# Where ScalarE makes a weight piece's top bits: between d and gh, or behind the piece's rounding

## The chip, the cores and the metric

The kernel runs on one core of one Trainium2 chip. The metric is the device time of one launch in microseconds (us). The three runs of the kernel before took 845.73, 847.87 and 848.03 us, the median is 847.87 us. The names of the engines are those of the profile: PE is TensorE, DVE is VectorE, ACT is ScalarE, POOL is GpSimd, SP is SyncE, whose queue issues the loads.

## The reference

Three layers follow one another, all in float32. The first is attention with a decay instead of a softmax; the second a feed-forward layer with the activation h·tanh(softplus(h)); the third sends each of the 2304 tokens to one of eight experts with a fixed capacity.

```
ret = (scale * q @ k.T) * Dmat ; x = ret @ v          # 4 x 8 heads, 576 x 64
h = x @ w_in                                          # 2304 x 512 @ 512 x 2048
g = h * tanh(log1p(exp(h))) ; y = g @ w_out           # 2048 -> 512
out[mask_e] = relu(y[mask_e] @ w1[e]) @ w2[e]         # 8 experts, 288 tokens each
```

## The kernel before, in words

Float32 products are made of split halves: a high part rounded to the matmul format (names ending in h) and the rest (ending in l), so each product is three matmuls. The second layer works in steps. A step is one block of 256 tokens (n) and one 128-wide slice f of the 2048 hidden units; there are 144 steps (9 blocks of 16 slices). In step i the program issues, in the order in which it is written:

- TensorE: twelve matmuls of h into the PSUM tile ph (L317), pieces of the attention that `slots` puts on this step (steps 0 to 9 carry many), and at the end the six matmuls of the output for the step three before (L411).
- ScalarE: tanh, square and scaling of ph into d (L326, L327, L328), and gh, the rounded high part of the activated value of the step two before (L358).
- VectorE: a product r of the two halves of d (L334), gl, the rest of gh (L359), a reciprocal (L339), u of the step before times ph (L352), and u of this step (L344). While weights are being made gl is on VectorE, later on GpSimd.

In the first 31 steps the weights of the second layer are also made, one piece of 128x512 a step. There are 32 pieces, half from w_in (winh, winl) and half from w_out (woh, wol). A piece arrives as 64-bit words (tile raw), and passes through six instructions of the class `convert`:

- `x1` on ScalarE, L159: makes the piece's top bits in the lower words of raw.
- `c` on ScalarE, L156: copies the upper word, scaled, into one of two buffers (y0).
- `x` on VectorE, L163: puts the sign into the top bits.
- `a` on VectorE, L168: joins top bits and copy. Behind it `fetch` issues the load of a later piece (L140, on SP's queue) into the raw buffer that has become free; raw has two buffers for most pieces, so it is the piece two further on.
- `h` on ScalarE, L174: the rounding, which gives the high part of the weights.
- `l` on GpSimd, L177: the rest.

A piece begins with `x1` and `c` in one step, has `x`, `a` and `h` in the next, and `l` in the one after (in the program; GpSimd starts it when the rounding is done). So a step's ScalarE work belongs to two pieces: `h` of one (`now`), `x1` and `c` of the next (`nxt`). No piece begins in step 20. Four pieces (0 to 3) begin ahead of the loop, 28 inside it. Each engine works through its own queue in order. Other VectorE work in the steps with attention is pm (L224) and xl (L255), other GpSimd work are two products on att (L228, L233), other ScalarE work xh (L254) and sd (L285).

Of the kernel before, what the change touches and what calls it, by code (L numbers as in the profile page):

```python
# [57 lines left out]
CONV = [i for i in range(80) if i < ALL or int((i + 1) * RATE) > int(i * RATE)]  # L58
# [23 lines left out]
def first_part(ctx, tc, att, att_ht, att_hn, dtab, qtab, ktab, stab, wi, wo, wgb, ydram, L, constants, cst, begin, grid):  # L82
# [59 lines left out]
    class convert:  # L142
# [18 lines left out]
        def x(self):  # L161
            w0 = self.w0
            nc.vector.scalar_tensor_tensor(w0, self.w1, 0x80000000, w0, op0=ALU.bitwise_and,  # L163
                                           op1=ALU.bitwise_or)
# [144 lines left out]
    def ff_h(n, f, i):  # L309
        xh, xl = x_block(n)  # L310
        if i % 2 == 0:
            hbank[0] = psum.tile([P, 2, TB], F32, tag=("ph0", "ph1")[i // 2 % 2], name="ph")
        ph = hbank[0][:, i % 2, :]
        k = 0
        for kt in range(KT):
            for w, x in ((winh, xh), (winl, xh), (winh, xl)):
                nc.tensor.matmul(ph, w[f][:, kt, :], x[:, kt, :], start=(k == 0), stop=(k == 11))  # L317
                k += 1
        q2[n, f] = ph

    def ff_a1(n, f, i, alone):

        ph = q2[n, f]
        d = work.tile([P, 2, P], F32, tag="d", name="d", bufs=2)
        df = d.rearrange("p a b -> p (a b)")
        nc.scalar.activation(df, ph, AF.Tanh, scale=0.5)  # L326
        nc.scalar.activation(df, df, AF.Square, bias=half_b, scale=-0.5)  # L327
        nc.scalar.activation(df, df, AF.Copy, bias=0.5, scale=0.5)  # L328
        u = work.tile([P, 2, P], F32, tag="u", name="u", bufs=3)
        r = u[:, 0, :]  # L330
        if alone:

            r = work.tile([P, DM], BF, tag="scr", name="r").bitcast(F32)[:, :P]
        nc.vector.tensor_mul(r, d[:, 0, :], d[:, 1, :])  # L334
        inv[n, f] = (d, u, r, alone)

    def ff_a2(n, f):
        r = inv[n, f][2]
        nc.vector.reciprocal(r, r)  # L339

    def ff_b1(n, f, eng):
        d, u, r, alone = inv.pop((n, f))
        if alone:
            eng.tensor_mul(u, d[:, ::-1, :], r[:, None, :].to_broadcast([P, 2, P]))  # L344
        else:
            eng.tensor_mul(u[:, 1, :], d[:, 0, :], r)  # L346
            eng.tensor_mul(u[:, 0, :], d[:, 1, :], r)  # L347
        gt[n, f] = u.rearrange("p a b -> p (a b)")

    def ff_b2(n, f):  # L350
        g = gt[n, f]
        nc.vector.scalar_tensor_tensor(g, g, -1.0, q2.pop((n, f)), op0=ALU.add, op1=ALU.mult)  # L352

    def ff_b3(n, f, eng):
        g = gt[n, f]
        gh = work.tile([P, TB], F32R, tag="gh", name="gh", bufs=3)
        gl = work.tile([P, TB], F32R, tag="gl", name="gl", bufs=3)
        nc.scalar.activation(gh, g, AF.Copy)  # L358
        eng.tensor_sub(gl, g, gh.bitcast(F32))  # L359
        gt[n, f] = (gh, gl)  # L360
# [152 lines left out]
    old, now, nxt = c2, c3, convert()  # L513
# [17 lines left out]
    for i in range(len(steps) + YL):  # L531
        new = i < len(steps)
        if i == 20:
            constants()
        if i == 62:
            stage.__exit__(None, None, None)
            late = tc.tile_pool(name="late", bufs=1)
            WG = late.__enter__().tile([P, E, DM], F32, name="WG")
            nc.sync.dma_start(WG, wgb)
        if now:  # L540
            now.x()
            now.a()
        if old:
            old.l()
        if new:
            n, f = steps[i]
            ff_h(n, f, i)
            for x in slots.get(i, []):
                x()
            ff_a1(n, f, i, bool(now or old))  # L550
        if nxt and i in CONV:
            nxt.x1()
        if new:

            eng = nc.vector if now or old else nc.gpsimd
            if i > 1:
                ff_b3(*steps[i - 2], eng)
            ff_a2(n, f)
            if i:
                ff_b2(*steps[i - 1])  # L560
            ff_b1(n, f, nc.vector if i == len(steps) - 1 else eng)
        if i == len(steps) - 1:
            ff_b2(n, f)
            ff_b3(*steps[i - 1], nc.gpsimd)
            ff_b3(n, f, nc.vector)
        if now:
            now.h()
        old, now = now, None
        if nxt and i in CONV:
            now, nxt = nxt, convert() if done[0] < len(parts) else None  # L570
            now.c()
        for k in range(2 if i % 4 == 0 or TAIL <= i < POP2 else 1):
            if idle:
                idle.pop(0)()
        if late and i > TAIL + BEGIN and not idle:
            late = late.__exit__(None, None, None)
            soon.extend(begin())
        if i >= YL:
            ff_y(*steps[i - YL], i)
# [840 lines left out]
def build(tc, ap, out):  # L1420
    nc = tc.nc
    with ExitStack() as ctx:
        pp = ctx.enter_context(tc.tile_pool(name="pp", bufs=1))
        dp = ctx.enter_context(tc.tile_pool(name="dp", bufs=1, space=bass.MemoryType.DRAM))
        cp = ctx.enter_context(tc.tile_pool(name="cp", bufs=1))
        ctx.enter_context(tc.manual_schedule())
        L = pp.tile([P, NT, E], F32, name="L")
        ydram = dp.tile([N, DM], F32, name="ydram")
        cst = {}
        start = []  # L1430
        cs = ExitStack()

        def begin():
            start.append(Search(cs, tc, L, cst))
            return start[0].early()

        with ExitStack() as c1:
            first_part(c1, tc, ap["att"], ap["att_ht"], ap["att_hn"], ap["dtab"], ap["qtab"],
                       ap["ktab"], ap["stab"], ap["wi"], ap["wo"], ap["wgb"], ydram, L, lambda: constants(cp, tc, ap, cst), cst, begin, lambda *a: Grid(cs, tc, L, cst).pieces(*a))
        keep = ctx.enter_context(tc.tile_pool(name="keep", bufs=1, reuse_waits="tile"))  # L1440
        L0 = keep.tile([P, NT, E], F32, name="L0")
        nc.gpsimd.tensor_copy(L0, L)
        with ExitStack() as c2:
            flag = second_part(c2, tc, L, ydram, ap["wx"], cst, out, start[0], True, L0)
            again = nc.values_load(flag[0:1, 0:1], min_val=0, max_val=1)
        cs.close()
        with tc.If(again != 0):
            with ExitStack() as c3:
                general_constants(c3, tc, ap, cst)
                second_part(c3, tc, L0, ydram, ap["wx"], cst, out, Start(c3, tc, L0, cst), False)  # L1450
# [15 lines left out]
def constants(cp, tc, ap, cst):  # L1466
    nc = tc.nc
    load_constants(cp, tc, ap, cst, (("ident", [P, P], F32), ("J", [P, NJ + 1], F32), ("SCL", [P, 3], F32),
                                     ("pri", [P, E], F32), ("tri", [P, P], BF), ("io", [P, 96], BF),
                                     ("pcv", [P, NT, 2], BF), ("WGN", [P, KT, E], F32)))  # L1470
    cst["ones"] = cp.tile([P, P], BF, name="c_ones")
    nc.vector.memset(cst["ones"], 1.0)
# [69 lines left out]
```

## Time and profile before

| | us |
|---|---|
| median of three runs | 847.87 |
| profiled execution, its own time | 849.51 |
| its span in the trace | 847.60 |
| PE busy | 776.6 (92%) |
| DVE busy | 548.1 (65%) |
| ACT busy | 437.3 (52%) |
| POOL busy | 475.1 (56%) |
| first and last L159 begin | 10.3, 156.3 |

Busy shares are means over the span. The stage in which weights are made is the first fifth of it, and there VectorE is the busiest engine, not TensorE. From the span's start to 170 us, DVE was busy for 135.67 us and PE for 134.16 us; behind that PE is busy nearly all the time.

### The profile page before, as it was taken

What the parts mean: (1) busy time and instruction counts of PE and PEld (TensorE: products, weight loads), DVE (VectorE), ACT (ScalarE), POOL (GpSimd) and SP (SyncE); (2) the same over time, 40 slices, a digit from 0 to 9 for tenths busy, and PEclk for the clock granted to TensorE, in tenths of its full rate; (3) what the DMA queues carried; (4) which work ended last, traced back from release to release, by engine and by line L of the source; (5) the groups of instructions that cost most, each with busy time, mean ns of one, the idle gap of its engine ahead of it and who ended that gap; (6) DMA issues with size and microseconds to landing.
All of it is one profiled execution on the core that took longest, in us unless ns stands there. A gap on an engine that the chain in (4) does not pass through costs nothing.

```text
span 847.6 us, 16248 instructions
## 1 busy us (share of the span) xinstructions
PE 776.6 (92%) x6151; PEld 709.3 (84%) x6151; DVE 548.1 (65%) x1271; ACT 437.3 (52%) x963; POOL 475.1 (56%) x541
## 2 busy tenths in 40 slices
PE   6688878899999999999999999939999999999993
PEld 5677667788998888888888889929989899999993
DVE  4797989865545699797897885576566654442110
ACT  2677878754554545455455554423444543554520
POOL 2533333365544567676666665414777986977811
PEclk9799999999999999999999999958999999999997
DMA  8536343101204210120110000044555655655411
GB/s 313 174 111 201 137 135 125 50 27 51 75 26 150 76 50 26 61 82 34 51 50 26 1 26 2 2 147 163 171 181 178 194 168 174 177 159 175 128 30 32
DMA packets 27320, 87.63 MB, mean 103 GB/s; under 512 B 4448, under 2 KB 5600, under 8 KB 27104
## 3 DMA queue, kind: packets, MB, share of 16 engines
q1 hardware_dynamic: 24160, 77.06, 27.9%
q0 software_dynamic: 3072, 9.44, 3.5%
q8 instruction: 50, 0.82, 0.4%
q14 instruction: 38, 0.31, 0.1%
HBM read 77.05 MB, written 9.44 MB: 102 GB/s over the span
## 4 chain that ended last, share of the span: by engine, by line
PE 72%; DVE 9%; issue 6%; DMA 5%; ACT 4%; POOL 2%; SPq 0%; DVEq 0%; POOLq 0%; ACTq 0%
PE ph L317 20%; PE hp L1257 10%; PE op L1271 8%; PE b_E L411 8%; PE b_F L411 7%; DMA raw<-in_wi_dram 2%; PE cnt L972 2%; PE b_A L219 1%; DVE r L339 1%; PE b_D L248 1%; DVE raw L163 1%; DVE hot L868 1%; POOL wxl L811 1%; DMA raw<-in_wo_dram 1%; PE b_E L447 1%
## 5 line engine op out<-in xcount | busy, mean ns | idle before, releaser
L317 PE MATMUL ph<-xh,winh 128*128 128x256 f32 x576 | 164.9, 286 | 9.4 <-ACT d L326 6.7
L317 PE MATMUL ph<-xl,winh 128*128 128x256 f32 x576 | 162.9, 283 | 0.2 <-DVE xl L255 0.2
L317 PE MATMUL ph<-xh,winl 128*128 128x256 f32 x576 | 163.0, 283 | 0.0
L811 POOL TENSOR_TENSOR wxl<-wraw,wxh 128x1024 fp32r<-128x1024 f32 x60 | 142.4, 2396 | 30.5 <-ACT wxh L809 30.0
L359 POOL TENSOR_TENSOR gl<-u,gh 128x256 fp32r<-128x256 f32 x114 | 85.8, 753 | 88.3 <-ACT gh L358 87.6
L317 PEld LDWEIGHTS ph<-xh,winh 128*128 128x128 f32 x576 | 110.4, 192 | 20.2 <-ACT d L326 7.0
L326 ACT ACTIVATE d<-ph 128x256 f32<-128x256 f32 x144 | 54.8, 381 | 133.0 <-PE ph L317 117.3
L317 PEld LDWEIGHTS ph<-xh,winl 128*128 128x128 f32 x576 | 110.8, 192 | 4.5
L317 PEld LDWEIGHTS ph<-xl,winh 128*128 128x128 f32 x576 | 111.1, 193 | 0.4 <-DVE xl L255 0.4
L339 DVE RECIPROCAL u<-u 128x128 f32<-128x128 f32 x113 | 107.7, 953 | 3.9
L334 DVE TENSOR_TENSOR u<-d 128x128 f32<-128x128 f32 x113 | 45.4, 402 | 63.3 <-ACT d L328 55.5
L346 POOL TENSOR_TENSOR u<-d,u 128x128 f32<-128x128 f32 x112 | 52.3, 467 | 52.9 <-DVE u L339 52.8
L809 ACT ACTIVATE wxh<-wraw 128x1024 fp32r<-128x1024 f32 x64 | 67.3, 1052 | 18.5 <-DMA wraw<-in_wx_dram 18.5
L327 ACT ACTIVATE d<-d,half_b 128x256 f32<-128x256 f32 x144 | 73.5, 510 | 4.7
L347 POOL TENSOR_TENSOR u<-d,u 128x128 f32<-128x128 f32 x112 | 68.2, 609 | 8.8
L328 ACT ACTIVATE d<-d 128x256 f32<-128x256 f32 x144 | 60.2, 418 | 4.6
L358 ACT ACTIVATE gh<-u 128x256 fp32r<-128x256 f32 x144 | 57.9, 402 | 2.1 <-DVE u L352 2.0
L368 DVE SCALAR_TENSOR_TENSOR scr<-y,WG 128x512 bf16<-128x512 f32 x64 | 55.2, 863 | 0.4
L1248 DVE SCALAR_TENSOR_TENSOR htl<-hp,hth 128x288 fp32r<-128x288 f32 x64 | 28.4, 454 | 40.2 <-ACT hth L1260 37.9
L1260 ACT ACTIVATE hth<-hp 128x288 fp32r<-128x288 f32 x64 | 26.1, 408 | 51.9 <-PE hp L1257 46.7
L352 DVE SCALAR_TENSOR_TENSOR u<-u,ph 128x256 f32<-128x256 f32 x144 | 52.5, 365 | 0.3
L177 POOL TENSOR_TENSOR wol<-y,woh 128x512 fp32r<-128x512 f32 x16 | 20.6, 1288 | 53.5 <-ACT woh L174 53.5
(271 smaller groups left out, 1931.0 us busy)
## 6 DMA issues: line engine op xcount, KB each, us to landing
wraw<-in_wx_dram SPq DMA_DIRECT2D x64, 512.0 KB, 4.4
att<-in_att_dram SPq DMA_DIRECT2D x32, 512.0 KB, 5.4
raw<-in_wi_dram SPq DMA_DIRECT2D x16, 512.0 KB, 3.9
raw<-in_wo_dram SPq DMA_DIRECT2D x16, 512.0 KB, 3.2
ydram<-y SPq DMA_DIRECT2D x9, 512.0 KB, 2.8
WG<-in_wgb_dram SPq DMA_DIRECT2D x1, 2048.0 KB
att<-in_att_ht_dram SPq DMA_DIRECT2D x4, 256.0 KB, 4.4
att<-in_att_hn_dram SPq DMA_DIRECT2D x4, 256.0 KB, 4.8
```

Of the source, the lines that this page charges most:

```text
L317: nc.tensor.matmul(ph, w[f][:, kt, :], x[:, kt, :], start=(k == 0), stop=(k == 11))
L327: nc.scalar.activation(df, df, AF.Square, bias=half_b, scale=-0.5)
L328: nc.scalar.activation(df, df, AF.Copy, bias=0.5, scale=0.5)
L339: nc.vector.reciprocal(r, r)
L347: eng.tensor_mul(u[:, 0, :], d[:, 1, :], r)
L358: nc.scalar.activation(gh, g, AF.Copy)
L359: eng.tensor_sub(gl, g, gh.bitcast(F32))
L411: nc.tensor.matmul(py[n][t], g[:, t * P:(t + 1) * P], w[f], start=(f == 0 and w is woh and g is gh), stop=(f == NF - 1 and g is gl))
L809: nc.scalar.activation(hi, raw, AF.Copy)
L811: rest = lambda eng: eng.tensor_sub(lo, raw, hi.bitcast(F32))
L1257: nc.tensor.matmul(hp, W[kt][w][:, s], x[:, kt, :], start=(k == 0), stop=(k == 11))
L1271: nc.tensor.matmul(op, W[4 + ft // 2][w][:, s], h[:, ft, :], start=(k == 0), stop=(k == 23))
```

## The change

In the loop, `x1` of the next piece is issued right in front of that piece's `c`, behind `h` of the present one. It was issued behind d and in front of gh.

```
@@ -548,8 +548,6 @@
             ff_a1(n, f, i, bool(now or old))
-        if nxt and i in CONV:
-            nxt.x1()
         if new:
             eng = nc.vector if now or old else nc.gpsimd
             if i > 1:
                 ff_b3(*steps[i - 2], eng)
...
         if now:
             now.h()
@@ -568,6 +566,7 @@
         if nxt and i in CONV:
             now, nxt = nxt, convert() if done[0] < len(parts) else None
+            now.x1()
             now.c()
```

On ScalarE's queue, in step 5: L327 and L328 are the last two of d, L159 is `x1` (in place in raw), L358 is gh, L174 the rounding of the present piece into woh, L156 the copy of the next one's upper word into a y0 buffer.

```order
 L327 ACTIVATE d<-d,half_b 128x256
 L328 ACTIVATE d<-d 128x256
-L159 ACTIVATE raw<-raw 128x512
 L358 ACTIVATE gh<-u 128x256
 L174 ACTIVATE woh_111<-y_153 128x512
+L159 ACTIVATE raw<-raw 128x512
 L156 ACTIVATE y_153<-raw 128x512
```

The top bits moved back past gh and the rounding, and stand between the rounding and the copy. All 28 pieces of the loop move in this way.

On VectorE's queue the instructions keep their order, and what they wait for is printed behind them. Here is the end of one early step and the beginning of the next: L344 is u, L163 is `x`, L168 is `a`, L255 is xl of the attention; Activation means ScalarE, DMAHW a load.

```order
 L352 SCALAR_TENSOR_TENSOR u<-u,ph 128x256
 L344 TENSOR_TENSOR u<-d,r 128x256 [waits DVE_49]
-L163 SCALAR_TENSOR_TENSOR raw<-raw 128x512 [waits DMAHW4_49]
+L163 SCALAR_TENSOR_TENSOR raw<-raw 128x512 [waits DMAHW4_49,Activation_49]
 L168 SCALAR_TENSOR_TENSOR y_153<-y_153,raw 128x512 [waits DVE_49,Activation_49]
 L255 TENSOR_TENSOR xl_608<-b_E,xh_607 128x4x64 [waits Activation_49]
```

L163 now waits for ScalarE by itself; before, the wait of L359 for gh, which stood behind the top bits, had covered it. 26 of the L163 gain this wait. The queues of PE, POOL and SP read the same as before.

## Rows read from the trace of the kernel before

**Rows 1.** Windows view, 170 to 620 us: window, length, busy time of each engine.
```profile
170.00:620.00 450.00, 432.61 (x3401) 392.29 (x3400) 322.91 (x716) 221.55 (x524) 260.88 (x378) 0.97 0.19 63
```
**Rows 2.** Chain that ended last, 80 to 125 us: start, length, what.
```profile
86.39 3.26 DMA raw<-in_wi_dram
...
117.96 4.51 DMA raw<-in_wi_dram
```
**Rows 3.** Groups of instructions, 80 to 163 us: busy, mean ns, idle before.
```profile
L359 DVE TENSOR_TENSOR gl<-u,gh 128x256 fp32r<-128x256 f32 x21 | 8.9, 424 | 5.1 <-ACT gh L358 4.9
...
L159 ACT ACTIVATE raw<-raw 128x512 uint32<-128x512 uint16 x19 | 12.8, 673 | 10.1 <-DMA raw<-in_wi_dram 5.5 <-DMA raw<-in_wo_dram 4.6
```
**Rows 4.** Timeline of ACT from 86 us: start, length, instruction, idle before.
```profile
86.40 0.63 ACT L174 ACTIVATE winh<-y 128x512 fp32r<-128x512 f32 x1 [0.37 <-DVE y L168]
86.93 0.65 ACT L156 ACTIVATE y<-raw 128x512 f32<-128x512 f32 x1
...
88.43 0.42 ACT L328 ACTIVATE d<-d 128x256 f32<-128x256 f32 x1
89.67 0.67 ACT L159 ACTIVATE raw<-raw 128x512 uint32<-128x512 uint16 x1 [0.82 <-DMA raw<-in_wi_dram]
90.25 0.40 ACT L358 ACTIVATE gh<-u 128x256 fp32r<-128x256 f32 x1
```
**Rows 5.** Timeline of DVE, one step from 85.67 us.
```profile
85.67 0.69 DVE L168 SCALAR_TENSOR_TENSOR y<-y,raw 128x512 uint32<-128x512 uint32 x1
86.28 0.29 DVE L334 TENSOR_TENSOR r<-d 128x128 f32<-128x128 f32 x1
86.48 0.42 DVE L359 TENSOR_TENSOR gl<-u,gh 128x256 fp32r<-128x256 f32 x1
...
87.96 0.71 DVE L344 TENSOR_TENSOR u<-d,r 128x256 f32<-128x256 f32 x1
88.59 0.68 DVE L163 SCALAR_TENSOR_TENSOR raw<-raw 128x512 uint32<-128x512 uint32 x1
89.38 0.69 DVE L168 SCALAR_TENSOR_TENSOR y<-y,raw 128x512 uint32<-128x512 uint32 x1
```
**Rows 6.** Timeline of POOL in the same step.
```profile
87.11 1.28 POOL L177 TENSOR_TENSOR winl<-y,winh 128x512 fp32r<-128x512 f32 x1 [2.43 <-ACT winh L174]
```
**Rows 7.** Timeline of DVE, later L168 and one L359.
```profile
120.95 0.69 DVE L168 SCALAR_TENSOR_TENSOR y<-y,raw 128x512 uint32<-128x512 uint32 x1
...
126.41 0.69 DVE L168 SCALAR_TENSOR_TENSOR y<-y,raw 128x512 uint32<-128x512 uint32 x1
...
130.43 0.43 DVE L359 TENSOR_TENSOR gl<-u,gh 128x256 fp32r<-128x256 f32 x1 [0.58 <-ACT gh L358]
...
133.03 0.69 DVE L168 SCALAR_TENSOR_TENSOR y<-y,raw 128x512 uint32<-128x512 uint32 x1
...
160.17 0.69 DVE L168 SCALAR_TENSOR_TENSOR y<-y,raw 128x512 uint32<-128x512 uint32 x1
```
**Rows 8.** Timeline of ACT, end of step 1.
```profile
35.93 0.65 ACT L159 ACTIVATE raw<-raw 128x512 uint32<-128x512 uint16 x1
36.48 0.61 ACT L174 ACTIVATE woh<-y 128x512 fp32r<-128x512 f32 x1
```
**Rows 9.** Timeline of POOL, behind that rounding.
```profile
38.39 1.48 POOL L228 TENSOR_TENSOR att<-att,qt 128x512 f32<-128x512 f32 x1
```
**Rows 10.** Timeline of DVE, r of step 2 and gl in step 9.
```profile
43.00 1.04 DVE L334 TENSOR_TENSOR r<-d 128x128 f32<-128x128 f32 x1
...
82.81 0.43 DVE L359 TENSOR_TENSOR gl<-u,gh 128x256 fp32r<-128x256 f32 x1 [0.56 <-ACT gh L358]
```
**Rows 11.** Timeline of all engines, 66 to 69 us, three of its rows.
```profile
66.27 1.30 POOL L228 TENSOR_TENSOR att<-att,qt 128x512 f32<-128x512 f32 x1 [0.71 <-PE b_D L219]
...
66.55 1.57 DVE L168 SCALAR_TENSOR_TENSOR y<-y,raw 128x512 uint32<-128x512 uint32 x1
...
68.86 0.47 PE L411 MATMUL b_C<-woh,gh 128*128 128x512 f32 x1 [2.77 <-ACT raw L159]
```

More of the change, by code (lines that the diff above doesn't have):

```diff
@@ L550, in first_part @@
             ff_a1(n, f, i, bool(now or old))
-        if nxt and i in CONV:
-            nxt.x1()
         if new:
@@ L570, in first_part @@
             now, nxt = nxt, convert() if done[0] < len(parts) else None
+            now.x1()
             now.c()
```

## The prediction, before the changed kernel had run

> **What bounds the kernel now.** I read the windows by stage first. Behind 170 us TensorE is the bound, busy for 432.61 of 450 us [rows 1], and nothing there depends on when the first stage ended. So what the first stage saves is passed on to the end, one for one.
>
> Next the chain of waits, inside the first stage. Between 80 and 160 us it is a loop over two steps: a weight load lands, the top bits (L159) start, gh follows on ScalarE, gl on VectorE, then the rest of VectorE's step, the next step's `x` and `a`, and behind `a` the next load; the chain holds such loads of 3.26 and, once, 4.51 us [rows 2].
>
> Third the groups of that stretch. Top bits waited 10.1 us for loads, and gl waited 4.9 us for gh, with ScalarE's queue held by the top bits [rows 3]. The timeline shows one case: d was done at 88.85 (88.43 + 0.42), the load held the top bits till 89.67, gh came at 90.25 [rows 4]. gh needs nothing of that load.
>
> Last one VectorE step in which nothing was late, 85.67 to 89.38: 3.71 us from `a` to `a` [rows 5]. What sets its length is seen with GpSimd's row beside it. `a` ends at 86.36 (85.67 + 0.69), the rounding starts at 86.40 [rows 4], GpSimd's rest of the piece runs from 87.11 to 88.39 [rows 6], and VectorE's u (L344), begun at 87.96, ends at 88.67, 0.28 behind GpSimd's end; `x` and `a` follow [rows 5]. So u is held while GpSimd runs, and the loop `a`, rounding, rest, u, `x`, `a` gives the 3.71.
>
> The Trainium skill has this as a rule: in "SBUF — State Buffer", section "SBUF: two separate sides", VectorE and GpSimd share a pair of ports as an exclusive lock, and a VectorE operation with two SBUF inputs that comes second is blocked until the GpSimd operation is done. Row and rule agree here; were the hold only a slower read, the step could go under 3.71, which is the fourth rival below.
>
> **The change part by part.** It moves 28 top-bit instructions and adds or removes none. TensorE, GpSimd and SP keep their queues.
>
> *What goes:* gh and the rounding no longer stand behind a load, and are earlier by at least the 0.58 us (90.25 − 89.67) that a top-bit instruction takes of ScalarE [rows 4].
>
> *What comes in its place:* the 0.58 is now behind the rounding. From the rounding's start to the end of d it was 2.45 us (86.40 to 88.85); with the top bits in between it is 3.03 us, so d of the next step is done 3.07 us behind the end of `a` (0.04 to start). VectorE asks for it 3.63 us behind (3.71 less the 0.08 by which r at 86.28 overlaps `a`): 0.56 us to spare [rows 4, 5]. These are paid for by ScalarE's idle time.
>
> *The load:* it is issued as `a` ends. The top bits of that piece now start behind the next rounding, 3.71 + 0.04 + 0.53 (86.40 to 86.93) = 4.28 us later. A load of 3.26 us has landed by then; one of 4.51 is 0.23 late, inside the 0.56 to spare [rows 2, 4].
>
> So I expect each step from 85 us on to take 3.71 us. The terms:
>
> - 85.67 to 120.95, nine steps [rows 5, 7]: 35.28 us, nine of 3.71 are 33.39. Gain 1.89.
> - 120.95 to 126.41, one step, the one with the 4.51 load: 5.46 − 3.71 = 1.75.
> - 126.41 to 133.03, two steps, one without a piece: gl's wait of 0.58 at 130.43 goes [rows 7]. TensorE also has work there, so only 0.58.
> - 133.03 to 160.17, seven steps [rows 7]: 27.14 − 25.97 = 1.17.
>
> Together 5.39. In the steps with attention (to 83 us) the loads are not late; there the gain is only the shift of 0.55 or so:
>
> - Step 1: the rounding's input is long ready, and it starts at 35.93 in place of 36.48 [rows 8]. GpSimd's rest of the piece and the attention product right behind it (38.39) move with it [rows 9], and VectorE's u, `x` and `a` there are held by these two and by the product after. Gain 0.55.
> - Step 9: gl's wait of 0.56 at 82.81 goes [rows 10]: d, gh, gl are the chain there. Gain 0.56.
> - Steps 7 and 8: `a` at 66.55 takes 1.57 us in place of 0.69, since GpSimd's product began at 66.27; behind it TensorE idles 2.77 us till 68.86 [rows 11]. VectorE's waits for gh in steps 3 to 6 go too, so `a` should move by more than the 0.28 that it needs to come first. If it does, up to 0.88 of VectorE's time goes, and TensorE idles less. Bounds 0, and 3 us (the 2.77 and a little); I take the middle, 1.5, since both the order of two starts and the price are open.
>
> *The new wait of `x`:* 26 of them wait for ScalarE. `x` comes after u, 2.2 us behind the end of `a`; the top bits end 0.04 + 0.53 + 0.67 = 1.24 behind it, so the wait is met. The bare cost of one: `a`, which waits for two engines, starts 0.11 behind the end of `x` (89.27 to 89.38), while gl, which waits for ScalarE, starts 0.09 before r ends (86.48, 86.57) [rows 5]. So between 0 and 26 × 0.11 = 2.9 us. I take 0: gl is the like case.
>
> Sum: 5.39 + 0.55 + 0.56 + 1.5 = 8.0 us. The profiled execution took 849.51 us and would take 841.5; set on the median of the runs, which is 1.6 lower, 847.87 − 8.0 = 839.9 us. Its own range is 837 (all 3 us in steps 7 and 8, and 0.4 more in the step pair at 130) to 844.3 (none there, and the 2.9 for waits: 6.5 − 2.9 = 3.6).
>
> **The rivals.**
>
> *The load still sets the step.* The wait moves with the top bits to a place in front of the copy and the next d. For: the load is in the chain of every second step. Against: 4.28 us from issue to need, and only one load of the stretch took longer. It decides once loads take over 4.28 + 0.56 = 4.84 us. Then the 5.39 is lost and 0.55 + 0.56 stay: 846.8. Chance 0.07.
>
> *The gain is given back at the stage's end.* If TensorE were the bound from some step before 160 us, the last 1.17 and 0.58 and part of the rest would only move its idle time. Against: the chain between the two loads of rows 2 has no TensorE in it, and TensorE idled 2.77 us in an earlier step of the stage [rows 11]. Some 3 us lost of 6.5 and nothing in steps 7 and 8: 844.4; half more lost: 846. Chance 0.07.
>
> *GpSimd comes ahead of r and gl (slower).* The rounding, and with it GpSimd's rest, moves ahead more than VectorE does in steps where pm or xl stand between `a` and r. Then r, with two SBUF inputs, is held: r at 43.00 took 1.04 us in place of 0.29 [rows 10]. Price per step up to the whole of L177, 1.28 [rows 6]. It decides where the rest starts before gl, which in the step of rows 5 and 6 starts 0.63 ahead of it (86.48, 87.11). In nine steps with attention this would be 11.5 us against the 6.5 gained: 847.87 + 5.0 = 852.9. For: one such step is there already. Against: in most of those steps gl is directly behind gh, and gh still precedes the rounding. Chance 0.04.
>
> *More than forecast.* u escapes the hold where VectorE gets to it before GpSimd starts, or the hold is not exclusive; steps of 3.42 us (u as short as gl, which has as many elements, 0.42 for 0.71 [rows 5]) in the 17 steps of the terms, 17 × 0.29 = 4.9 us more: 835.0. Against: the row says 0.28 behind GpSimd's end. Chance 0.05.
>
> **How the numbers follow.** The forecast has 0.77, the rivals 0.07, 0.07, 0.04 and 0.05. A change under 0.3% (2.5 us) can't be told from none: 845.3 to 850.4 is "same". The forecast's own range lies below it, save a tail of 0.03. Faster: 0.77 − 0.03 + 0.05 + about 0.05 of the first two rivals = 0.84; same 0.12; slower 0.04. The range reaches down to 836.5 for half of the last rival, and up to 845.5.
>
> **What would show it.** In the profile after: L159 without waits for loads between 85 and 160 us; L359 without waits for gh; `a` to `a` 3.71 us in nearly every step, with u ending 0.28 behind L177; the last L168 at about 152 instead of 160.17; behind it the same profile, shifted. I am wrong if r (L334) waits for d in those steps, which would say that ScalarE's tail is too long; if L159 still waits, in its new place; or if `a` at 66 us is still held, which costs 1.5 of the sum.

## The result, and the profile after

| | before | changed |
|---|---|---|
| median of 5 runs | 847.87 us (845.73 to 848.03) | 840.91 us (837.51 to 842.78) |
| ratio of the runs, 95% interval | | 0.9914 (0.9892 to 0.9936) |
| profiled execution / its span | 849.51 / 847.6 us | 837.55 / 835.5 us |
| last join L168 of the first stage starts | 160.17 us | 149.00 us |

The changed kernel is faster by 6.96 us; 8.0 were forecast. Its profiled execution is one of the fastest of its runs, so it shows more than the median. Two repeats of it in other batches, with profiles of their own, show the common case (they are the first and the last experiment).

I read the profile after in the order of the prediction. The groups of instructions between 85 and 160 us of the changed kernel (busy us, mean ns, idle before and its releaser):

```profile
L159 ACT ACTIVATE raw<-raw 128x512 uint32<-128x512 uint16 x17 | 11.2, 657 | 0.0
...
L359 DVE TENSOR_TENSOR gl<-u,gh 128x256 fp32r<-128x256 f32 x19 | 7.9, 418 | 0.0
L174 ACT ACTIVATE woh<-y 128x512 fp32r<-128x512 f32 x10 | 6.3, 633 | 4.4 <-DVE y L168 4.4
```

Top bits (L159) had waited 10.1 us for loads and gl (L359) 4.9 us for gh [rows 3]; both wait for nothing now. ScalarE's wait has moved to the rounding (L174), and its releaser is the join L168: ScalarE is early and waits for VectorE. One step of ScalarE's timeline in the changed kernel:

```profile
87.28 0.40 ACT L358 ACTIVATE gh<-u 128x256 fp32r<-128x256 f32 x1
88.08 0.63 ACT L174 ACTIVATE winh<-y 128x512 fp32r<-128x512 f32 x1 [0.40 <-DVE y L168]
88.62 0.65 ACT L159 ACTIVATE raw<-raw 128x512 uint32<-128x512 uint16 x1
89.16 0.66 ACT L156 ACTIVATE y<-raw 128x512 f32<-128x512 f32 x1
...
90.67 0.42 ACT L328 ACTIVATE d<-d 128x256 f32<-128x256 f32 x1
90.99 0.40 ACT L358 ACTIVATE gh<-u 128x256 fp32r<-128x256 f32 x1
```

Rounding, top bits, copy, and gh directly behind d; in [rows 4] the top bits stood between d and gh with 0.82 us of waiting for the load. d is done at 91.09 (90.67 + 0.42) and VectorE's next r starts at 91.68: 0.59 to spare, where 0.56 had been worked out. VectorE in the same step:

```profile
87.36 0.69 DVE L168 SCALAR_TENSOR_TENSOR y<-y,raw 128x512 uint32<-128x512 uint32 x1
...
89.64 0.71 DVE L344 TENSOR_TENSOR u<-d,r 128x256 f32<-128x256 f32 x1
90.28 0.68 DVE L163 SCALAR_TENSOR_TENSOR raw<-raw 128x512 uint32<-128x512 uint32 x1
91.07 0.69 DVE L168 SCALAR_TENSOR_TENSOR y<-y,raw 128x512 uint32<-128x512 uint32 x1
```

and GpSimd's rest of the piece:

```profile
88.79 1.29 POOL L177 TENSOR_TENSOR winl<-y,winh 128x512 fp32r<-128x512 f32 x1 [2.42 <-ACT winh L174]
```

From join to join 3.71 us, and u ends at 90.35, 0.27 behind GpSimd's 90.08: the undisturbed step of [rows 5, 6], now in nearly every step. The joins that answer to [rows 7], later in VectorE's timeline of the changed kernel:

```profile
79.94 0.69 DVE L168 SCALAR_TENSOR_TENSOR y<-y,raw 128x512 uint32<-128x512 uint32 x1
...
113.34 0.69 DVE L168 SCALAR_TENSOR_TENSOR y<-y,raw 128x512 uint32<-128x512 uint32 x1
117.14 0.69 DVE L168 SCALAR_TENSOR_TENSOR y<-y,raw 128x512 uint32<-128x512 uint32 x1
123.04 0.69 DVE L168 SCALAR_TENSOR_TENSOR y<-y,raw 128x512 uint32<-128x512 uint32 x1
...
149.00 0.69 DVE L168 SCALAR_TENSOR_TENSOR y<-y,raw 128x512 uint32<-128x512 uint32 x1
```

The join at 79.94 is that of step 10 and answers to the one at 85.67. From there to the last it was 74.50 us and is 69.06. The other gains of this execution lie ahead of it: 3.00 us from step 7's join to step 10's, 2.64 from step 1's to step 7's. Behind the stage it is the same profile, shifted: from the first step without a piece (165.62 before, 154.45 after) to the end of the span it took 681.98 and 681.05 us.

### The profile page after: what moved, and what is told of

It reads as the page before. It is cut to its first block, busy times and chain, and to the rows that moved or that the text cites. A ratio compares the mean times of both kernels' runs of the same rounds, so it can differ in the third digit from the quotient of the medians.

```text
span 835.5 us, 16274 instructions
## 1 busy us (share of the span) xinstructions
PE 771.1 (92%) x6151; PEld 702.5 (84%) x6151; DVE 546.5 (65%) x1271; ACT 437.5 (52%) x963; POOL 475.3 (57%) x541
## 4 chain that ended last, share of the span: by engine, by line
PE 69%; DVE 15%; issue 7%; ACT 3%; POOL 3%; DMA 2%; SPq 0%; DVEq 0%; POOLq 0%; ACTq 0%
PE ph L317 20%; PE hp L1256 9%; PE op L1270 8%; PE b_E L411 8%; PE b_F L411 7%; DVE r L339 3%; DVE raw L163 2%; DVE u L344 2%; PE cnt L971 2%; PE b_A L219 2%; PE b_D L248 1%; DVE hot L867 1%; PE b_E L447 1%; DVE y L168 1%; POOL wxl L810 1%
## 5 line engine op out<-in xcount | busy, mean ns | idle before, releaser
L359 POOL TENSOR_TENSOR gl<-u,gh 128x256 fp32r<-128x256 f32 x114 | 85.7, 752 | 89.4 <-ACT gh L358 88.6
L808 ACT ACTIVATE wxh<-wraw 128x1024 fp32r<-128x1024 f32 x64 | 67.4, 1053 | 17.4 <-DMA wraw<-in_wx_dram 17.4
L327 ACT ACTIVATE d<-d,half_b 128x256 f32<-128x256 f32 x144 | 73.5, 510 | 4.7
L328 ACT ACTIVATE d<-d 128x256 f32<-128x256 f32 x144 | 60.2, 418 | 4.6
L358 ACT ACTIVATE gh<-u 128x256 fp32r<-128x256 f32 x144 | 57.9, 402 | 2.1 <-DVE u L352 2.0
L1256 PE MATMUL hp<-xth,wxh 128*128 128x288 f32 x256 | 50.1, 309 | 0.9 <-DVE htl L1247 0.9
```

The source lines that it names most:

```text
L808: nc.scalar.activation(hi, raw, AF.Copy)
L1256: nc.tensor.matmul(hp, W[kt][w][:, s], x[:, kt, :], start=(k == 0), stop=(k == 11))
```

## The experiments

All were timed over five rounds, beside the kernel before on the same chip. Steps are named by their join. (The texts of the first batch call the joins at 85.67 and 79.94 those of step 11; they are step 10's, as in the prediction.) One table first, since most verdicts rest on the same three stretches of each profile; "step 7" is the length of its join, 0.69 us when it runs free.

| kernel | median us | ratio (95%) | steps 7 to 10 | step 10 to last | step 7's join |
|---|---|---|---|---|---|
| before | – | – | 19.12 | 74.50 | 1.57 |
| changed, first profile | 840.91 | 0.9914 (0.9892–0.9936) | 16.12 | 69.06 | 0.69 |
| changed, second | 841.92 | 0.9918 (0.9903–0.9932) | 18.84 | 69.08 | 1.80 |
| changed, third | 841.87 | 0.9926 (0.9904–0.9947) | 18.82 | 69.07 | 1.80 |
| new place from step 10 on | 844.28 | 0.9945 (0.9929–0.9960) | 19.05 | 69.07 | 1.57 |
| new place up to step 9 | 844.25 | 0.9949 (0.9932–0.9966) | 16.13 | 73.28 | 0.69 |
| old place, no loads | 843.62 | 0.9941 (0.9927–0.9956) | 18.79 | 69.65 | 1.57 |
| between gh and rounding | 844.25 | 0.9967 (0.9955–0.9979) | 19.05 | 71.12 | 1.57 |

**The changed kernel again.**

> The changed kernel once more, for a second profile. Theory (the load's wait is taken out of gh's way): from the step after the attention on, every step is 3.71 us from L168 to L168, so the last L168 stands about 69.0 us behind the one that opens step 11 (79.94 to 149.00 in the first profile), in this profile too; what differs between executions lies ahead of 80 us or behind 155 us. Rival (the stage's gain is a matter of TensorE's clock in that execution): the 69 us differ as well, by 1 us or more. Time 837.5 to 843 us by both.

The ratio and the 69.08 us repeat. What doesn't repeat is step 7: its join was held again, and 2.7 us of the first profile are not there. That is taken up by the later experiments.

**One half of the change at a time.** The new place only from step 10 on, in the line of the call (the second kernel has the two conditions swapped):

```diff
+        if nxt and i in CONV and i < 10:
+            nxt.x1()
...
-            now.x1()
+            if not (i < 10):
+                now.x1()
```

> Only the steps from 10 on have the new order, steps 0 to 9 the old one. Theory: the steps of 3.71 us and with them 5.4 us of gain come from the late loads of the late steps, so 69.0 us from the L168 of step 11 to the last one (74.5 us before), and 842.5 us in all. Rival (the gain comes from the attention steps, by the rounding's shift and the clock): 847 us, since nothing is changed there.

> Only steps 0 to 9 have the new order, the later ones the old one. Theory: 2.6 us of gain (0.55 in step 1, 0.56 in step 9, 1.5 or up to 3 around step 7), 845.3 us; the L168 that begins at 66.55 us is no longer held by GpSimd and takes 0.69 us; from the L168 of step 11 to the last one it is 74.5 us as before. Rival (attention steps): the whole gain is here, 841 us.

The late half alone gives the 69.07 us of the whole change, with L159's waits gone from that stretch. Its group from 85 to 150 us:

```profile
L159 ACT ACTIVATE raw<-raw 128x512 uint32<-128x512 uint16 x17 | 11.1, 655 | 0.0
```

The early half alone leaves 73.28 us there. So the loads' part of the gain is where the prediction put it. Its size is less sure: 73.28 is 1.22 less than in before, though both have the old order from step 10 on, so what the loads cost there isn't fixed, and the 5.4 us are taken against one profile of before. Each half is worth about 0.5% by itself, more together than the 0.8% of both, because the early half's gain depends on step 7, which ran free in its profile.

**No load to wait for, old order.** Pieces 10 to 31 take the data of an earlier piece's buffer and issue no load; the true weights of these pieces are left out:

```diff
         if len(raws) < len(parts):
             i = len(raws)
+            if i >= 10:
+                raws.append(raws[i - 2])
+                return
```

> The old order, but pieces 10 to 31 have no load: each takes the words of the piece two before it, so the weights are not the right ones and the output isn't the reference's. Theory (it is the load that held gh through the top bits): with no load to wait for, the old order also runs at 3.71 us a step, and the last L168 stands 69 to 69.6 us behind that of step 11 (74.5 before); the stage gains 5 us. Rival (it is the 0.58 us of the top bits themselves in front of gh and the rounding): 74 us, since the order is the old one. Read by the stage; the time in all can differ, as other tokens go to other experts.

With the order of before and no load, ScalarE's timeline has the old order without the wait:

```profile
90.30 0.42 ACT L331 ACTIVATE d<-d 128x256 f32<-128x256 f32 x1
90.63 0.67 ACT L162 ACTIVATE raw<-raw 128x512 uint32<-128x512 uint16 x1
91.20 0.40 ACT L361 ACTIVATE gh<-u 128x256 fp32r<-128x256 f32 x1
```

(L159, L331 and L361 of this kernel stand three lines further down than in before.) The stretch is 69.65 us, 4.85 of the 5.44 gained. It is the load that cost the time, not the 0.57 us of ScalarE between d and gh.

**Half way: between gh and the rounding.** gh is freed of the load, the rounding is not:

```diff
+        if nxt and i in CONV:
+            nxt.x1()
         if now:
             now.h()
...
-            now.x1()
             now.c()
```

> The top bits stand between gh and the rounding: gh is ahead of the load, the rounding behind it. Theory (two things were held by the load: gl through gh, and the loop rounding, GpSimd's rest, u, x, a through the rounding): gl waits no more, but the rounding waits for the load and the top bits, so a loop over two steps of 3.29 (load) + 0.58 + 0.70 (rounding) + 1.29 (rest) + 0.28 - 0.09 + 0.79 + 0.69 = 7.53 us, 3.77 a step; from the L168 of step 10 to the last one 70 to 70.5 us against 69.1; 842 to 843 us in all. Rival (only gl's wait for gh mattered): 69.1 as in the changed kernel, 841.5 us.

ScalarE's timeline in that kernel:

```profile
87.53 0.40 ACT L358 ACTIVATE gh<-u 128x256 fp32r<-128x256 f32 x1
88.40 0.69 ACT L159 ACTIVATE raw<-raw 128x512 uint32<-128x512 uint16 x1 [0.46 <-DMA raw<-in_wi_dram]
88.98 0.62 ACT L174 ACTIVATE woh<-y 128x512 fp32r<-128x512 f32 x1
```

71.12 us: freeing gh takes 3.38 of the 5.44, freeing the rounding the other 2.06. I had 70 to 70.5 for it; the loads still held the rounding in more steps than thought, 7.6 us of waits in the group of L159 (18 of them).

**What sets the 3.71: GpSimd out of the step.** The rest of a piece is replaced by a fill with zeros, so the low parts of the weights are left out:

```diff
-            nc.gpsimd.tensor_sub(self.lo, self.t, self.hi.bitcast(F32))
+            nc.gpsimd.memset(self.lo.bitcast(F32), 0.0)
```

> The changed kernel, in which GpSimd fills a piece's rest (L177) with zeros and reads nothing: the low parts of the weights are left out, so the output is less exact. Theory (u is held by GpSimd's reads till they end, and the loop through the rounding and the rest is what sets 3.71): u takes 0.41, a step is 3.4 us, and from the L168 of step 10 to the last one it is 64 us against 69.1; 836 us in all. Rival (VectorE's own work sets the 3.71, or ScalarE's): 69 us and 841.5 us.

The total, 1237.87 us, says nothing about the stage: with these weights the experts' layer behind it runs twice (its groups at L808 and L1256 have twice as many instructions, and the program has 23173 for 16274). The stage can be read. The fills depend on nothing and ran far ahead, so GpSimd is idle in these steps. VectorE:

```profile
86.52 0.69 DVE L168 SCALAR_TENSOR_TENSOR y<-y,raw 128x512 uint32<-128x512 uint32 x1
...
88.81 0.41 DVE L344 TENSOR_TENSOR u<-d,r 128x256 f32<-128x256 f32 x1
89.14 0.68 DVE L163 SCALAR_TENSOR_TENSOR raw<-raw 128x512 uint32<-128x512 uint32 x1
89.92 0.69 DVE L168 SCALAR_TENSOR_TENSOR y<-y,raw 128x512 uint32<-128x512 uint32 x1
...
93.16 0.69 DVE L163 SCALAR_TENSOR_TENSOR raw<-raw 128x512 uint32<-128x512 uint32 x1 [0.53 <-ACT raw L159]
```

u takes 0.41 in place of 0.71 and the step 3.40: the hold of u is what the 3.71 is made of. And with a shorter step the load is back: `x` waits 0.53 us for the top bits in the next one. Even so the stretch was 64.73 us.

**A shorter hold.** If GpSimd must begin later than the end of the whole rounding, two halves let it begin after the first:

```diff
-            nc.scalar.activation(self.hi, self.t, AF.Copy)
+            for k in range(2):
+                c = slice(256 * k, 256 * k + 256)
+                nc.scalar.activation(self.hi[:, c], self.t[:, c], AF.Copy)
...
-            nc.gpsimd.tensor_sub(self.lo, self.t, self.hi.bitcast(F32))
+            for k in range(2):
+                c = slice(256 * k, 256 * k + 256)
+                nc.gpsimd.tensor_sub(self.lo[:, c], self.t[:, c], self.hi[:, c].bitcast(F32))
```

> The changed kernel with the rounding (ScalarE) and the rest (GpSimd) of a piece each in two halves of 256 columns, so that GpSimd can begin after half the rounding. Theory (rounding, rest, u, x, a are the loop): GpSimd ends 0.2 to 0.3 us earlier, a step is 3.45 to 3.55 us, 65 to 66.5 us from the L168 of step 10 to the last one against 69.1, and 838 us in all. Rival (VectorE or ScalarE set the step; ScalarE gets one more fixed cost a step): 69.5 to 70 us, 842.5 us.

GpSimd and VectorE in one step of it:

```profile
89.38 1.44 POOL L181 TENSOR_TENSOR winl<-y,winh 128x256 fp32r<-128x256 f32 x2 [2.21 <-ACT winh L176]
90.44 0.65 DVE L348 TENSOR_TENSOR u<-d,r 128x256 f32<-128x256 f32 x1
```

836.62 us, ratio 0.9894 (0.9862 to 0.9926), and 67.84 us from step 10 to the last join, 3.64 a step. The start came 0.2 us earlier, but the two halves took 1.44 us where one instruction took 1.28, so most of it went again; u still ends 0.27 behind GpSimd's end (90.82, 91.09). The 3.45 to 3.55 expected had left out the price of the second instruction. The time in all is more than this stretch explains: it gives 1.2 us against the changed kernel's 69.07, and the join of step 7 ran free in this profile (0.69 us, steps 7 to 10 in 16.05), which it did not in the two repeats of the changed kernel.

**Step 7, first try: the attention products on VectorE.** They hold the join there, so those of the first seven chunks leave GpSimd:

```diff
-            nc.gpsimd.tensor_mul(qT, qT, Q_[:, :, :n])
+            (nc.vector if ci < 7 else nc.gpsimd).tensor_mul(qT, qT, Q_[:, :, :n])
```

(and the same for the product of kn.)

> The changed kernel with GpSimd's two products of the attention on VectorE for the first seven chunks (those of steps up to 9). Theory (in step 7 L168 and GpSimd's product start within 0.01 us of one another, and the loser waits; that decides 3 to 4 us): with no such product on GpSimd L168 takes 0.69 us in every execution, and so do x, a and r in steps 2 and 5, for 0.4 to 0.7 us more VectorE work a product; the L168 of step 10 stands 53.5 us or less behind that of step 0 in every profile (53.65 and 57.72 in two of the changed kernel); 838.5 us in all and a smaller spread. Rival (VectorE's 5 us of added work make the first ten steps longer): 843 us.

847.16 us, ratio 1.000 (0.9989 to 1.0011): the theory missed. No join is held any more, but VectorE now carries the products, and r is held by GpSimd's rest of the piece. From step 0's join to step 10's it took 60.61 us, against 53.65 to 57.72 in the three profiles of the changed kernel. Two rows of VectorE in it:

```profile
55.41 0.41 DVE L228 TENSOR_TENSOR att<-att,qt 128x256 f32<-128x256 f32 x1
55.74 1.36 DVE L334 TENSOR_TENSOR r<-d 128x128 f32<-128x128 f32 x1
```

**Step 7, second try: who comes first.** A copy of one column on GpSimd, which needs the join's output, stands ahead of step 7's products:

```diff
+        if ci == 6:
+            nc.gpsimd.tensor_copy(behind, now.t[:, 0:1])
         if s0 > 0:
             nc.gpsimd.tensor_mul(qT, qT, Q_[:, :, :n])
...
+    behind = big.tile([P, 1], F32, name="behind")
     half_b = big.tile([P, 1], F32, name="half_b")
```

> The changed kernel, in which GpSimd, ahead of its products of the attention in step 7, copies one column of what that step's L168 writes, so that the product can't start before L168 is done. Theory (in step 7 the two race for the shared reads, and the loser's 1.1 to 1.8 us turn into 3 to 4 us by the chain through pm, TensorE and d): L168 takes 0.69 us in step 7 in each execution, the L168 of step 10 stands 53 to 55 us behind that of step 0 (53.65 where L168 came first, 57.72 where it came second), and the time is that of the better executions of the changed kernel, 838 us, within 2 us. Rival (the spread of the early steps is TensorE's clock, the race only a sign of it): a median like the changed kernel's, 841 us, and 56 to 58 us in the profile though L168 isn't held.

GpSimd, VectorE and TensorE around that join:

```profile
64.73 0.69 DVE L168 SCALAR_TENSOR_TENSOR y<-y,raw 128x512 uint32<-128x512 uint32 x1
...
65.48 0.18 POOL L228 COPY behind<-y 128x1 f32<-128x1 f32 x1 [1.75 <-DVE y L168]
...
66.17 0.47 PE L413 MATMUL b_C<-woh,gh 128*128 128x512 f32 x1 [1.60 <-DVE pm L224]
```

The join ran free and TensorE idled 1.60 us in place of 2.73, and steps 7 to 10 took 16.23 us. Yet the total was 842.73, ratio 0.9943 (0.9928 to 0.9958), and not 838. The stage ended as early as it should, but from there to the end of the span it took 686.0 us where it had been 681 to 683.

**Both, with another cut.** The same copy, and rounding and rest in parts of 128 and 384 columns.

```diff
+CUTS = (slice(0, 128), slice(128, 512))
...
-            nc.scalar.activation(self.hi, self.t, AF.Copy)
+            for c in CUTS:
+                nc.scalar.activation(self.hi[:, c], self.t[:, c], AF.Copy)
...
-            nc.gpsimd.tensor_sub(self.lo, self.t, self.hi.bitcast(F32))
+            for c in CUTS:
+                nc.gpsimd.tensor_sub(self.lo[:, c], self.t[:, c], self.hi[:, c].bitcast(F32))
```

> The same, with the rounding and the rest in two unequal parts, 128 and 384 columns. Theory (a GpSimd part starts as soon as the first part of the rounding is done, and u, x, a and the rounding follow its end): GpSimd ends 0.1 us earlier than with halves, 3.55 us a step, 66 us from the L168 of step 10 to the last one (67.8 with halves, 69.1 in one piece), and 835 us in all, 3 us under the run with L168 ordered alone. Rival (the second part of the rounding is late, or ScalarE's tail now sets the step): 3.65 to 3.75 us a step and 837 us or more.

839.72 us, ratio 0.9909 (0.9892 to 0.9925). Step 10 to last: 66.56 us, 3.54 a step, as expected, the shortest stage so far; but 685.0 us behind it, so the 835 us expected in all were not reached. These two share what the kernel with two halves has not: the copy and its 4-byte tile `behind`.

**The changed kernel a third time**, for step 7.

> The changed kernel a third time, beside the two above. Theory (race in step 7): 841 us median, and the profile falls in one of two kinds: L168 of step 7 takes 0.69 us and the L168 of step 10 stands 53 to 55 us behind that of step 0, or it takes 1.6 to 1.8 us and the distance is 57 us or more. Rival (clock): distances in between, without regard to whether L168 was held.

GpSimd, VectorE and TensorE at step 7 of it:

```profile
63.89 1.27 POOL L228 TENSOR_TENSOR att<-att,qt 128x512 f32<-128x512 f32 x1 [0.99 <-PE b_D L219]
63.90 1.80 DVE L168 SCALAR_TENSOR_TENSOR y<-y,raw 128x512 uint32<-128x512 uint32 x1
...
66.45 0.47 PE L411 MATMUL b_C<-woh,gh 128*128 128x512 f32 x1 [2.73 <-DVE pm L224]
...
67.03 1.50 DVE L359 TENSOR_TENSOR gl<-u,gh 128x256 fp32r<-128x256 f32 x1
```

and in the first profile of the same kernel:

```profile
63.82 0.69 DVE L168 SCALAR_TENSOR_TENSOR y<-y,raw 128x512 uint32<-128x512 uint32 x1
63.82 1.83 POOL L228 TENSOR_TENSOR att<-att,qt 128x512 f32<-128x512 f32 x1 [0.99 <-PE b_D L219]
...
65.26 0.47 PE L411 MATMUL b_C<-woh,gh 128*128 128x512 f32 x1 [1.61 <-DVE pm L224]
```

Join and product start within 0.01 us of each other, and one of the two is held: the join for 1.80 us, or the product for 1.83. In before GpSimd was 0.28 ahead [rows 11], and the join lost there and in the three other profiles with the old order in these steps (1.57 us each). The change brought it to a draw. Where the join wins, steps 7 to 10 take 16.1 us, where it loses 18.8. In the three profiles it won once; it won in the one profile of the early half too.

The held join is only the first part of this price. TensorE's matmul of the output (L411) waits for pm, which stands behind the join: 2.73 us in the third profile and 1.61 in the first. After the longer wait the granted clock falls. From 68 to 70 us, in the windows view of the third profile (window, length, busy time of each engine, granted clock, DMA):

```profile
68.00:70.00 2.00, 2.00 (x10) 1.81 (x9) 2.00 (x5) 0.00 (x0) 0.24 (x1) 0.50 0.93 252
```

and of the first:

```profile
68.00:70.00 2.00, 2.00 (x13) 1.76 (x13) 1.90 (x5) 1.57 (x4) 0.29 (x1) 1.00 0.93 262
```

0.50 is the lower of the clock's two levels, 1.2 of 2.4 GHz. From that matmul to step 8's products of att with sd (L243) TensorE took 7.25 us in the third profile (66.45 to 73.70) and 5.67 in the first (65.26 to 70.93). So of the 2.7 us some 1.1 are the longer wait, and 1.6 are TensorE at the lower level behind it. The other twelve profiles fall in the same two kinds: 6.92 to 7.27 us behind a wait of 2.73 to 3.48, in seven of them (before is one, and so is the kernel with the products on VectorE, in which no join is held), and 5.67 to 5.77 behind one of 1.47 to 1.61, in five. So the lower clock goes with the longer wait of TensorE, not with the held join as such; the copy, which only sets the order, took away both.

The third profile's 56.64 us from step 0 to 10 is just under the 57 expected of a held one; the difference is in step 1, which varies (below).

**The tile put elsewhere.** As the last combination, with the copy's tile at the end of the first stage's own pool, so that every other tile stands where it stands in the changed kernel:

```diff
-            nc.gpsimd.tensor_copy(behind, now.t[:, 0:1])
+            nc.gpsimd.tensor_copy(sp.tile([P, 1], F32, name="behind"), now.t[:, 0:1])
...
-    behind = big.tile([P, 1], F32, name="behind")
```

> The same kernel as the last combination (GpSimd's small copy ahead of step 7's products, rounding and rest split into 128 and 384 columns), but the 4-byte tile that the copy writes no longer stands in the pool of the weights: it stands at the end of the first stage's own pool, so that every other tile has the address that it has in the changed kernel. In the two kernels with that tile among the others, TensorE took 390.6 and 390.5 us from the first step behind the stage to the first count matmul, in before and the changed kernel 387.5; its matmuls of xh with winl had a mean of 282 instead of 279 ns. Theory that the shifted addresses cost this: 387.5 us again, 279 ns, the first stage as in the combination (52.6 us to step 10's join, 66.6 from there to the last), total about 836.5. Rival, that the copy or the split in itself costs it: 390.5 us again and about 839.7.

837.18 us (835.91 to 839.11), ratio 0.9870 (0.9855 to 0.9885). The largest group of TensorE behind the stage that changed, first in the kernel with the 4-byte tile among the weights (160 to 540 us):

```profile
L319 PE MATMUL ph<-xh,winl 128*128 128x256 f32 x440 | 124.0, 282 | 0.0
```

and then with that tile elsewhere:

```profile
L324 PE MATMUL ph<-xh,winl 128*128 128x256 f32 x436 | 121.7, 279 | 0.0
```

From the first step behind the stage (152.55) to the count matmuls that begin at 539.97 (below) it took 387.4 us, with the tile among the weights 390.6 and 390.5, in before 387.6:

```profile
539.97 1.30 PE L978 MATMUL cnt<-oh,ind 128*63 128x8 bf16 x18 [1.16 <-DVE ind L693]
```

The place of the tile cost the 3 us, not the copy and not the cut. This kernel is 1.3% faster than the one before, and its interval lies below those of both repeats of the changed kernel. It has the lowest ratio of the study; the interval of the two halves (0.9894, 0.9862 to 0.9926) overlaps with its own.

## Why the prediction was right, point by point

*The bound and the one-for-one.* Right. The stage's 11.17 us of the first profile reached the end, and 0.93 more; in the third profile the last join came 8.38 us earlier (at 151.79; "about 152" was forecast) and the span was 7.4 shorter, in the second 5.92 earlier (at 154.25) and 5.6 shorter.

*The loads held gh and the rounding* (5.39). Right in cause and size: 5.44, 5.42 and 5.43 in three profiles, against the one of before. Loads left out in the old order give 4.85, the late half of the change 5.43. By its parts: nine steps take 33.40 us where 33.39 were forecast, one takes 3.80 and not 3.71, seven take 25.96 for 25.97. Only the pair that ran from 126.41 to 133.03 was put too low: it was 6.62 us [rows 7] and is 5.90 (117.14 to 123.04), so the gain is 0.72 and not 0.58.

*u held by GpSimd sets 3.71.* Shown by the step of 3.40 without GpSimd's work. The rule of the Trainium skill in "SBUF — State Buffer", section "SBUF: two separate sides", gives the shared ports to whichever of the two operations starts first, for its whole length; step 7 agrees, where a start within 0.01 us decided which of the two took 1.8 us.

*ScalarE's 0.58, the load's 4.28, the wait of `x`.* Right, all covered: 0.59 us to spare, no wait for a load, and no step longer by a wait of `x`. Each cover is thin. In a step of 3.40 the top bits were late at once.

*Step 1* (0.55). Right, in place and size. The joins of steps 1 and 2 hide it, since r of step 1 waits for d for a time that varies. VectorE in before:

```profile
36.06 0.29 DVE L334 TENSOR_TENSOR r<-d 128x128 f32<-128x128 f32 x1 [2.27 <-ACT d L328]
...
40.53 1.35 DVE L168 SCALAR_TENSOR_TENSOR y<-y,raw 128x512 uint32<-128x512 uint32 x1
```

and in the changed kernel, first profile:

```profile
34.41 0.29 DVE L334 TENSOR_TENSOR r<-d 128x128 f32<-128x128 f32 x1 [0.71 <-ACT d L328]
...
38.35 1.34 DVE L168 SCALAR_TENSOR_TENSOR y<-y,raw 128x512 uint32<-128x512 uint32 x1
```

From r to step 2's join it took 4.47 to 4.49 us in the four profiles in which the top bits still stand ahead of the rounding there (before, the late half, half way, no loads), and 3.92 to 3.94 in the three of the change: 0.53 to 0.57 gained. The wait of r was 0.71 us where the granted clock from 26 to 44 us was 0.93, 1.01 to 1.66 where it was 0.77 to 0.82, and 2.12 and 2.27 where it was 0.72 and 0.74, in old and new order alike. The first profile had the shortest, 1.56 us less than before; that is no gain that the change can be shown to have made.

*A term put at nothing: steps 2 to 6.* From step 2's join to step 7's it took 26.02 to 26.06 us in those four profiles and 25.43 to 25.47 in the three of the change: 0.55 to 0.63 gained. The prediction saw that waits for gh go there, but used it only for the order of the two starts in step 7. (The early half alone had 23.91; there the granted clock from 44 to 66 us was 1.00, in the others 0.92.)

*Step 9* (0.56). This step failed. "gl's wait of 0.56 at 82.81 goes" was true, "d, gh, gl are the chain there" was not. ScalarE's xh (L254), which waits for TensorE, and sd stand ahead of d in this step. ScalarE's xh and VectorE's r in before:

```profile
78.23 0.60 ACT L254 ACTIVATE xh<-b_E 128x512 fp32r<-128x512 f32 x1 [1.35 <-PE b_E L248]
...
81.96 0.29 DVE L334 TENSOR_TENSOR r<-d 128x128 f32<-128x128 f32 x1 [2.01 <-ACT d L328]
```

and in the changed kernel, first profile, with VectorE's join and gl:

```profile
73.02 0.69 DVE L168 SCALAR_TENSOR_TENSOR y<-y,raw 128x512 uint32<-128x512 uint32 x1
...
73.06 0.60 ACT L254 ACTIVATE xh<-b_E 128x512 fp32r<-128x512 f32 x1 [1.26 <-PE b_E L248]
...
76.78 0.29 DVE L334 TENSOR_TENSOR r<-d 128x128 f32<-128x128 f32 x1 [2.40 <-ACT d L328]
77.09 0.42 DVE L359 TENSOR_TENSOR gl<-u,gh 128x256 fp32r<-128x256 f32 x1
```

gl follows r at once, but r, which had waited 2.01 us for d, now waits 2.40. From xh to r it is 3.73 us in before and 3.72 here. From join to join the step is 6.92, 7.02 and 7.27 us in the three profiles where it was 7.01: nothing gained. Behind xh there is a gain, 6.88 to 6.90 us to the next join where it was 7.44, but it is the earlier rounding's: half way, with gl directly behind r and the rounding still behind the top bits, it is 7.44 too. And it is given back ahead of xh, which started 0.43 us before the step's join and starts 0.04 to 0.37 behind it now: the join moved ahead by more than TensorE's part.

*Steps 7 and 8* (1.5, bounds 0 and 3). The bounds were right and the middle was never seen: with step 9 in the stretch it is 0.3 us (18.8 for 19.12) where GpSimd wins the draw and 3.0 (16.1) where the join wins. That the upper bound fits is in part luck: it stood for TensorE's idle 2.77 us "and a little", but where the join wins TensorE still idles 1.61, and 1.6 of the gain is the granted clock, which is in no term. "`a` should move by more than the 0.28 that it needs" was the weak sentence: GpSimd's product waits for TensorE's scores, which moved ahead too, and the two came out level. The draw is 2.7 us of the 6.5 and 4.7 by which the spans of the two repeats exceed the first profile's. How much of the spread of the changed kernel's runs (837.5 to 844.3 us) it makes stays open, since only three were profiled; the kernel before, with an order that lost it in every profile, spreads from 846.2 to 850.1 us in one batch by itself.

*The sum.* With the draw lost: 5.43, 0.3, 0.55 in step 1 and 0.6 in steps 2 to 6, 6.9 us; with it won 9.6. Counted from step 0's join to the last one and without the varying wait of r, the three profiles of the change gained 9.5, 6.8 and 6.8. The median's 6.96 is close to the lost draw. So the mechanism of the main term was right, and the 8.0 came near partly by luck: one term of 0.56 wasn't there, one of 0.6 was missing, and 1.5 stood for a draw between 0.3 and 3.0. The range was also miscounted: its lower end, with 1.5 and 0.4 more than 8.0, is 838.0 and not 837.

*The rivals.* The load setting the step, and the gain given back at the end, were not seen (no waits for loads; the same 681 to 683 us behind the stage). "GpSimd ahead of r and gl" is there, in one step and not in nine: gl at 67.03 takes 1.50 us for 0.42 in the held step 7. It is part of why a lost draw leaves only 0.3 of that term. Steps of 3.42 need GpSimd's work to be away, which the change doesn't do.

## What to carry to other kernels

An instruction that waits for a load belongs in an in-order queue behind everything that doesn't need the load, as long as its own result isn't needed sooner; what it costs where it stands is the wait that it passes on, not its own 0.6 us. Once such a wait is gone, look for the next loop before adding up: here a port hold set a floor of 3.71 us, and every gain was measured against that floor. When two engines start within a few hundredths of a microsecond on a shared port, price the change as one case or the other and not as their mean. Add a gain up only along what the step hangs on: a wait that goes is worth nothing where something else, here TensorE's b_E in step 9, comes no earlier. And if a tile is added for a trial, put it where it moves no other tile.

## What was not expected of the hardware

A tile of 4 bytes a partition in front of others in the pool made TensorE slower: the mean of 440 matmuls of xh with winl went from 279 to 282 ns, and the stretch behind the stage from 387.6 (before) to 390.6 us. Taking the tile elsewhere took it back. The matmuls of xl with winh stayed at 279 ns throughout; those of xh with winh went from 280 to 281 and 282. That it is the addresses of the operands, shifted by the tile, is the nearest reading; no run moved a single operand.

An instruction on GpSimd has a price apart from its columns: 512 columns took 1.28 us, two times 256 together 1.44, and 128 with 384 took 1.43 to 1.48, so about 0.15 to 0.2 us for the second one.
